# Attention and two feed-forward layers on one core: per-row factors spread by TensorE in the first pairs, Newton steps for the inverse root, weight words joined as integers, paced transfers

## The chip, the core and the metric

The kernel runs on one core of one Trainium2 chip. A core has five engines with an instruction queue each: TensorE (matrix products), VectorE, ScalarE, GpSimd, and SyncE, which here issues every transfer between memory and the on-chip buffers. In the rows they are called PE, DVE, ACT, POOL and SP; PEld is TensorE's weight load. Each engine works through its own instructions in the order in which they were written, and waits where an operand is not there yet. The metric is the device time of one execution in microseconds (us), as the median of several runs.

## What is computed

```
attention: 4 batches x 12 heads, 448 positions, head size 64
  q_n, k_n = rmsnorm(q, g_q), rmsnorm(k, g_k)       # x / sqrt(mean(x*x) + 1e-6) * g
  p = exp(s - max(s)),  s = q_n k_n^T / 8
  p = p / (sum(p) + 1e-9);  a = p v
x = a as 1792 rows of 768
x = relu(x @ w_in)**2 @ w_out                        # hidden size 2048
x = (silu(x @ w_gate) * (x @ w_val)) @ w_out2        # hidden size 1536
```

## The kernel before

**Attention.** Two heads of 448 rows are taken together as a pair and cut into 7 row tiles of 128; there are 24 pairs, six to a batch. For a pair the kernel loads k and q transposed (`kq`), scales k by its norm and by the gains, splits k and q each into a rounded part and a rest (`kst`, `kst_lo`, `qst`, `qst_lo`), and forms the scores of a tile with three products (`sc`, L678). VectorE takes the row maxima (L706) and forms the exponent's bias (`m`, L707); ScalarE takes the exponential and the row sum (`ring`, L720); TensorE turns the tile (`pt`, L777), a copy takes it out of PSUM (`turned_p`), and when all seven are there, eight products with v make the pair's output (`o`, L809). VectorE multiplies it by the inverse row sums (`ox`, L826). Pairs are numbered from 0, so o of pair 4 is the fifth.

**Norms.** `row_sums` loads the natural rows (`nat`), squares them and sums them (`ss`, L470). `rsqrt` makes the inverse root: VectorE adds the constant (L435) and GpSimd raises to the power -0.5 (L441), once for k (`stage`) and once for q (`rms`), for one or two pairs at a time. The factors of k lie along partitions but are needed along the free axis in all 128 partitions. For pair 0 TensorE turns them (`rows`, L557) and spreads them with a selecting matrix `pick` (`rk`, L522). For all other pairs they go to memory (`rkd`, L499) and are read back into 128 partitions (`rkb`, L602). The inverse row sums take the same way (`zd` L750, `zb` L758).

**Weights.** Every weight arrives as 64-bit words, of which the kernel makes a 32-bit number, and from that a rounded part and a rest. A half tile of 128 x 384 (a chunk) takes these steps in `load_weights`: scale the high word (`wa`, ScalarE or VectorE), then on VectorE a shift (L279), sign and bits joined (L282), exponent bits masked (L285), low word times exponent (L288), the sum (L292, VectorE or GpSimd), then the rounded part and the rest (`lo`, L305). There are 136 chunks, 24 of them for the first six blocks of the first layer, decoded during attention.

**Feed-forward.** Each product is three matrix products of 448 columns (L318). As soon as a batch's attention is done, parts of the first layer (`h_a`, `ya`) fill gaps between the attention's instructions (rank FILL); they are 702 matrix products in all, with the last batch's `lead`. After attention the sweeps of `products()` follow, which hold nothing but feed-forward work; between sweeps x is read back in six tiles, one after another (`xr`, L1042, then ScalarE's copy and VectorE's subtraction L1045).

**What sets the order.** The Python code plays a schedule before it writes instructions: every step is a generator that names the engines it could run on with a planned cost in ns; W is a VectorE step that shares a port with GpSimd, G a GpSimd step, S a transfer. `dispatch` hands each engine, whenever its planned clock is free, the ready job of lowest rank. So a changed cost or step moves all later instructions, on every engine, and a step that may run on two engines can change its engine. The two PSUM banks f0 and f1 are lent to attention until `LEND` tiles have their exponentials, and are then given to the filling work.

Of the kernel before, what the change touches and what calls it, by code (L numbers as in the profile page):

```python
# [9 lines left out]
F32 = mybir.dt.float32  # L10
# [18 lines left out]
EPS_SUM = 1e-9  # L29
RING = 6  # L30
LEND = 28
# [33 lines left out]
SIGN_EXP_BITS = -(1 << 23)  # L65
# [4 lines left out]
def attention_two_ffn_kernel(  # L70
# [112 lines left out]
    def dispatch(e):  # L183
# [15 lines left out]
        if e == "S":  # L199
            dma_free[0] = max(dma_free[0], clock[0] + 1100) + p[2] / 360  # L200
            done = dma_free[0] + 900
        else:
            done += p[2] if len(p) > 2 else settle[e]
# [9 lines left out]
    def dma(issue, nbytes):  # L213
        yield DMA_MARGIN
        yield {"S": 475}, issue, nbytes
# [34 lines left out]
    def load_weights(items):  # L250
# [7 lines left out]
        def chunk(key, place, c, raw_at):  # L258
# [33 lines left out]
            yield {"W": 469, "G": 956}, lambda e: e.tensor_tensor(out=t, in0=t, in1=a, op=ALU.add)  # L292
# [114 lines left out]
    pick = xp.tile([128, 2 * S], F32, tag="x5", name="pick")[:PT].rearrange("p (t m) -> p t m", t=PT)  # L407
    nc.gpsimd.memset(pick, 0.0)
    for i in range(PT):
        nc.gpsimd.affine_select(  # L410
            out=pick[:, i, :], in_=pick[:, i, :], compare_op=ALU.not_equal, fill=1.0, base=-i,
            pattern=[[0, 128]], channel_multiplier=1,
        )
# [16 lines left out]
    power = ap.tile([128, 2, PT], F32, name="power")  # L430
    nc.gpsimd.memset(power, -0.5)

    def rsqrt(ss, ends):

        yield {"W": 150}, lambda e: e.tensor_scalar(  # L435
            out=ss, in0=ss, scalar1=1.0 / D, scalar2=EPS_RMS, op0=ALU.mult, op1=ALU.add
        )
# [13 lines left out]
    def stat_tiles(b):  # L451
        for name, tag in (("ss", f"ss{b % 2}"), ("rms", f"rms{b % 2}")):
            stat[name, b] = ap.tile([128, 2, PB, PT], F32, tag=tag, name=f"{name}{b}")
# [29 lines left out]
    def stats(b, p, n):  # L483
# [4 lines left out]
        yield lambda: ("ss", b) in stat  # L488
# [4 lines left out]
        y, ss = (stat[name, b][:, :, p:p + n] for name in ("rms", "ss"))  # L493
        yield lambda: stage_free
        at = stage_free.pop(0)
        yield from rsqrt(ss, [(stage[at][:, :n * PT].rearrange("p (r t) -> p r t", t=PT), 0), (y[:, 1], 1)])
# [6 lines left out]
    def first_stats():  # L503
# [7 lines left out]
        rows, rows_at = yield from k_rows(0, 0, 1, 0)  # L511
        yield lambda: t_banks
        where = t_banks.pop(0)
        rk = tile_at(where, [128, S], F32, "rk")

        def broadcast(e):
            for h in range(2):
                at = 0
                while at < S:
                    i, c = divmod(h * S + at, 128)  # L520
                    w = min(128 - c, S - at)
                    e.matmul(  # L522
                        rk[64 * h:64 * h + 64, bass.ds(at, w)], lhsT=pick[:, i, :64], rhs=rows[:, c:c + w],
                        start=True, stop=True,
                    )
                    at += w

        yield {"P": 1500}, broadcast, 0
        spawn(first_k(rk, where), -95, True)
        rkr_free.append(rows_at)  # L530

    def row_sums_then(gen, w):
        yield from gen
        y, ss = (stat[name, 0][:, w, 0] for name in ("rms", "ss"))
        yield from rsqrt(ss, [(y if w else stage[0][:, :PT], None)])
        summed.add(w)
        if w:
            rms_ready.add(0)

    def first_k(rk, where):  # L540
        yield settle["P"]
        yield lambda: 0 in raw_kq and gained
        k = raw_kq[0][:, :S]
        yield {"W": 596}, lambda e: e.scalar_tensor_tensor(
            out=k, in0=k, scalar=gqk, in1=rk, op0=ALU.mult, op1=ALU.mult
        )
        ks[0] = [k]
        t_banks.append(where)

# [11 lines left out]
    ks, qs, vs, raw_kq, kq_at = {}, {}, {}, {}, {}  # L561
# [5 lines left out]
    def feed():  # L567

        for g in range(NH // 2):
# [17 lines left out]
            raw_kq[g] = kq if g in PLAIN else 2  # L587
# [5 lines left out]
            spawn(load_rk(g, kq[:, :S]), rank, True)  # L593
# [141 lines left out]
    def norms(g):  # L735
# [12 lines left out]
        sum_free.append(at)  # L748
        yield 200
# [69 lines left out]
    def pair_outputs(g, o, o_at):  # L819

        yield settle["P"]
        yield lambda: ox_free and g in zinv
# [4 lines left out]
        t_banks.append(o_at)  # L827
        zb_free.append(zb_at)
# [404 lines left out]
```

## Time and profile before

| | before |
|---|---|
| median of 3 runs, us | 1331.65 (1327.26 to 1337.62) |
| the profiled execution, us | 1334.34 |
| its span on the core, us | 1332.5 |
| TensorE busy, us and share of the span | 1281.5, 96% |
| VectorE busy | 756.2, 57% |
| ScalarE busy | 577.9, 43% |
| GpSimd busy | 196.4, 15% |
| mean granted TensorE clock | 0.985 |

The shares are means over stages that differ. In the first 200 us VectorE and ScalarE are close to full and TensorE has gaps; later TensorE hardly ever stops. Busy time of TensorE is not useful time: at the half clock a product is busy for longer, and matrix products overlap, so that their busy time is longer than their spacing.

### The profile page before, as it was taken

What the parts mean: (1) busy time and instruction counts of PE and PEld (TensorE: products, weight loads), DVE (VectorE), ACT (ScalarE), POOL (GpSimd) and SP (SyncE); (2) the same over time, 40 slices, a digit from 0 to 9 for tenths busy, and PEclk for the clock granted to TensorE, in tenths of its full rate; (3) what the DMA queues carried; (4) which work ended last, traced back from release to release, by engine and by line L of the source; (5) the groups of instructions that cost most, each with busy time, mean ns of one, the idle gap of its engine ahead of it and who ended that gap; (6) DMA issues with size and microseconds to landing.
All of it is one profiled execution on the core that took longest, in us unless ns stands there. A gap on an engine that the chain in (4) does not pass through costs nothing.

```text
span 1332.5 us, 18347 instructions
## 1 busy us (share of the span) xinstructions
PE 1281.5 (96%) x6565; PEld 1079.2 (81%) x6565; DVE 756.2 (57%) x1568; ACT 577.9 (43%) x1260; POOL 196.4 (15%) x156
## 2 busy tenths in 40 slices
PE   8888998999999999999999989999999999999998
PEld 5455555667668899999999979999999999999998
DVE  6888995455432899947943588221229961213122
ACT  6887887666763444523522243121215431211110
POOL 6674554433201000000000000000000000000000
PEclk9997999999999999999999989999999999999999
DMA  6565655432310544654453356120105420303021
GB/s 215 175 197 152 188 160 163 152 102 84 101 60 21 166 143 132 206 171 137 150 186 98 126 176 182 37 83 1 63 0 188 144 81 1 104 0 111 15 84 42
DMA packets 87421, 153.10 MB, mean 115 GB/s; under 512 B 15385, under 2 KB 66914, under 8 KB 87330
## 3 DMA queue, kind: packets, MB, share of 16 engines
q1 hardware_dynamic: 87330, 151.93, 36.9%
q8 instruction: 52, 0.85, 0.3%
q14 instruction: 39, 0.32, 0.1%
HBM read 122.82 MB, written 29.07 MB: 114 GB/s over the span
## 4 chain that ended last, share of the span: by engine, by line
PE 72%; DMA 3%; DVE 2%; ACT 1%; issue 1%; SPq 0%; POOL 0%; DVEq 0%; ACTq 0%
PE y L318 25%; PE h_v L318 13%; PE h_g L318 13%; PE h L318 11%; PE h_a L318 3%; PE ya L318 2%; PE pt L777 2%; PE o L809 2%; PE sc L678 1%; DMA xr<-x2d 1%; DMA raw_in<-in_w_in_dram 1%; DMA nat<-in_q_n_dram 0%; ACT ring L720 0%; DMA raw_out<-in_w_out_dram 0%; DMA zb<-zd 0%
## 5 line engine op out<-in xcount | busy, mean ns | idle before, releaser
L318 PE MATMUL h_g<-x,hi_g 128*128 128x448 f32 x576 | 165.2, 368 | 5.9 <-ACT x L209 5.9
L318 PE MATMUL h_v<-x,hi_v 128*128 128x448 f32 x576 | 165.8, 369 | 0.0
L318 PE MATMUL y<-s,hi_o 128*128 128x448 f32 x576 | 164.1, 366 | 0.0
L318 PE MATMUL y<-s,hi_out 128*128 128x448 f32 x552 | 159.3, 370 | 3.1 <-DVE r L355 3.1
L720 ACT ACTIVATE ring<-sc,m,rms 128x448 f32<-128x448 f32 x168 | 122.8, 733 | 58.8 <-PE pt L777 45.4
L318 PE MATMUL h<-x,hi_in 128*128 128x448 f32 x516 | 147.4, 367 | 0.0
L371 DVE TENSOR_TENSOR sig<-h_g,sig 128x448 f32<-128x448 f32 x48 | 29.9, 623 | 189.1 <-ACT sig L370 189.0
L777 PEld LDWEIGHTS pt<-ident,ring 128*128 128x128 f32 x672 | 75.4, 145 | 68.9 <-ACT turned_p L209 26.1
L777 PE MATMUL pt<-ident,ring 128*128 128x128 f32 x672 | 108.1, 291 | 21.1 <-ACT turned_p L209 11.7
L318 PEld LDWEIGHTS h_g<-x,hi_g 128*128 128x128 f32 x576 | 108.3, 188 | 15.8 <-ACT x L209 6.2
L706 DVE TENSOR_REDUCE sc<-sc 128x1 f32<-128x448 f32 (+1 forms) x96 | 93.8, 977 | 42.1 <-PE sc L678 36.1
L318 PEld LDWEIGHTS h_v<-x,hi_v 128*128 128x128 f32 x576 | 109.3, 190 | 9.5
L318 PEld LDWEIGHTS y<-s,hi_o 128*128 128x128 f32 x576 | 108.1, 188 | 9.3
L318 PEld LDWEIGHTS y<-s,hi_out 128*128 128x128 f32 x552 | 105.1, 191 | 12.5 <-DVE r L355 3.5
L370 ACT ACTIVATE sig<-h_g 128x448 f32<-128x448 f32 x48 | 26.2, 545 | 191.7 <-PE h_g L318 191.4
L318 PE MATMUL h_v<-x,lo_v 128*128 128x448 f32 x288 | 106.0, 368 | 0.0
L318 PE MATMUL h_g<-x,lo_g 128*128 128x448 f32 x288 | 105.6, 367 | 0.0
L318 PE MATMUL y<-s,lo_o 128*128 128x448 f32 x288 | 105.4, 366 | 0.0
L318 PEld LDWEIGHTS h<-x,hi_in 128*128 128x128 f32 x516 | 96.9, 188 | 8.6
L318 PE MATMUL y<-s,lo_out 128*128 128x448 f32 x276 | 101.9, 369 | 0.0
L209 ACT COPY turned_p<-pt 128x512 f32<-128x512 f32 x165 | 94.0, 588 | 5.2 <-PE pt L777 5.1
L318 PE MATMUL h<-x,lo_in 128*128 128x448 f32 x258 | 94.5, 366 | 0.0
(157 smaller groups left out, 2283.7 us busy)
## 6 DMA issues: line engine op xcount, KB each, us to landing
raw_in<-in_w_in_dram SPq DMA_DIRECT2D x32, 384.0 KB
raw_out<-in_w_out_dram SPq DMA_DIRECT2D x32, 384.0 KB
kq<-in_kq_p_dram SPq DMA_DIRECT2D x23, 480.0 KB
xr<-x2d SPq DMA_DIRECT2D x42, 224.0 KB
raw_g<-in_w_gate_dram SPq DMA_DIRECT2D x24, 384.0 KB
raw_v<-in_w_val_dram SPq DMA_DIRECT2D x24, 384.0 KB
raw_o<-in_w_out_dram SPq DMA_DIRECT2D x24, 384.0 KB
xr<-x1d SPq DMA_DIRECT2D x36, 224.0 KB
```

Source lines behind the costliest of these rows:

```text
L209: e.copy(out, src)
L318: return {"P": 203}, lambda e: e.matmul(ps, lhsT=w, rhs=x, start=first, stop=last), 0
L370: yield {"A": 424}, lambda e: e.activation(out=t, in_=pg, func=ACTF.Sigmoid)
L371: yield {"V": 535}, lambda e: e.tensor_tensor(out=t, in0=pg, in1=t, op=ALU.mult)
L678: e.matmul(parts[t][:, :S], lhsT=q[a][d, bass.ts(i % 4, 128)], rhs=k[c][d], start=(p == 0), stop=(p == len(passes) - 1),)
L706: e.tensor_reduce(out=top, in_=sc, axis=AX.X, op=ALU.max, negate=True)
L720: yield {"A": 704}, lambda e: e.activation(out=probs(at + t), in_=parts[t][:, :S], func=ACTF.Exp, bias=m[:, t:t + 1], scale=rq[:, i:i + 1] ...
L777: e.transpose(ps[:, bass.ts(j, 128)], p[:, bass.ds(min(128 * j, S - 128), 128)], ident)
L809: e.matmul(o[64 * h:64 * h + 64], lhsT=v[:, 4 * h + j], rhs=turned_p[:, 2 * j + h], start=(j == 0), stop=(j == 3),)
```

## The change

1. `SPREAD_K = 5`, `SPREAD_Z = 5`: the norms of k and the inverse row sums of pairs 0 to 4 are spread by TensorE with `pick` (now 14 rows wide) into a PSUM bank, and don't go through memory. `spread`, `spread_k` and `first_k` do it. For these pairs the output is first copied out of PSUM (`ox<-o`), so that its bank comes free before the factors are there.
2. `rsqrt` no longer raises to a power on GpSimd: it begins from an integer estimate and takes three Newton steps, all on VectorE for pairs 0 to 2 (three groups, `fused`: L436 to L451), otherwise with the beginning on VectorE and the steps on GpSimd (13 small instructions).
3. A chunk's words are joined as integers: the low word is scaled to its top three bits (L286), sign joined (L290), the high word shifted in (L293). The mask, the product and the sum are gone. The raw buffer is free after L286, and the sum can no longer go to GpSimd.
4. The planner's transfer rate goes from 360 to 300, and a transfer of 150000 bytes or more is not issued while the planned queue is more than 600 ns ahead. `LEND` goes from 28 to 35: one pair later.

```diff
-LEND = 28
+LEND = 35
+SPREAD_K = 5
+SPREAD_Z = 5
+DMA_RATE = 300
+DMA_BULK = 150000
+DMA_QUEUE = 600
...
     def dma(issue, nbytes):
         yield DMA_MARGIN
+        while nbytes >= DMA_BULK and dma_free[0] > clock[0] + 1100 + DMA_QUEUE:
+            yield dma_free[0] - clock[0] - 1100 - DMA_QUEUE
         yield {"S": 475}, issue, nbytes
...
             yield {"W": 269}, lambda e: e.tensor_scalar(
-                out=ti, in0=ai, scalar1=3, scalar2=None, op0=ALU.logical_shift_left
+                out=ti, in0=raw[:, :, 0].bitcast(U32), scalar1=2.0 ** -29, scalar2=7.0, op0=ALU.mult, op1=ALU.min
             )
+            raws.append(raw_at)
             yield {"W": 469}, lambda e: e.scalar_tensor_tensor(
                 out=ti, in0=ai, scalar=SIGN_BIT, in1=ti, op0=ALU.bitwise_and, op1=ALU.bitwise_or
             )
-            yield {"W": 269}, lambda e: e.tensor_scalar(
-                out=ai, in0=ti, scalar1=SIGN_EXP_BITS, scalar2=None, op0=ALU.bitwise_and
+            yield {"W": 469}, lambda e: e.scalar_tensor_tensor(
+                out=ti, in0=ai, scalar=3, in1=ti, op0=ALU.logical_shift_left, op1=ALU.bitwise_or
             )
-            yield {"W": 469}, lambda e: e.scalar_tensor_tensor(
-                out=a, in0=raw[:, :, 0].bitcast(U32), scalar=2.0 ** -52, in1=a, op0=ALU.mult, op1=ALU.mult
-            )
-            raws.append(raw_at)
-            yield {"W": 469, "G": 956}, lambda e: e.tensor_tensor(out=t, in0=t, in1=a, op=ALU.add)
             was.append(a_at)
...
-        for dst, part in ends:
-            src = ss if part is None else ss[:, part]
-            to = power[:, 0] if part is None else power[:, :src.shape[1]]
-            yield {"G": 900}, lambda e: e.tensor_tensor(out=dst, in0=src, in1=to, op=ALU.pow)
+        if fused:
+            def all_steps(e):
+                begin(e)
+                for i in range(3):
+                    step(e, ends if i == 2 else [(y, None)])
+
+            yield {"W": 170 * (10 + len(ends))}, all_steps
+            return
+        yield {"W": 300}, begin
+        for i in range(3):
+            yield {"G": 900}, lambda e: step(e, ends if i == 2 else [(y, None)])
...
-        yield from dma(lambda e: e.dma_start(out=rk_d[b][p * PT:(p + n) * PT, :], in_=rows), 0)
+        for r in range(n):
+            if b * PB + p + r < SPREAD_K:
+                yield from spread_k(b * PB + p + r, rows, r)
+        if b * PB + p + n > SPREAD_K:
+            yield from dma(lambda e: e.dma_start(out=rk_d[b][p * PT:(p + n) * PT, :], in_=rows), 0)
...
+    def spread(rows, parts, name):
+
         yield lambda: t_banks
         where = t_banks.pop(0)
-        rk = tile_at(where, [128, S], F32, "rk")
+        ps = tile_at(where, [128, S], F32, name)
...
+        yield {"P": 1100}, broadcast, 0
+        return ps, where
...
+        if g < SPREAD_Z:
+            parts = [(4 * h + t, 0, 128, h, 128 * t) for t in range(3) for h in range(2)]
+            parts += [(3, 64 * h, 64, h, 384) for h in range(2)]
+            zinv[g] = yield from spread(rows, parts, f"zb{g}")
+            zr_free.append(zr_at)
+            return
...
+        if g < SPREAD_Z:
+            yield {"A": 467, "V": 535}, lambda e: copy(e, ox, o)
+            t_banks.append(o_at)
+            o = ox
+            yield lambda: g in zinv
         zb, zb_at = zinv.pop(g)
         yield {"V": 535}, lambda e: e.tensor_tensor(out=ox, in0=o, in1=zb, op=ALU.mult)
```

What this does to the written order is seen at three places.

TensorE, from the last turned tile of pair 0 to pair 0's product with v, before (`sum` holds the inverse row sums, `stage` the k factors of later pairs; the first product of pair 1 stands behind o):

```order
L777 MATMUL pt_508<-ident,ring 128x128 x4
L557 MATMUL rows<-ident,sum_255 128x128
L557 MATMUL rows<-ident,stage_257 128x128
L809 MATMUL o_539<-turned_p,v_247 64x448 x8
L678 MATMUL sc_565<-kst_529,qst_361 128x448
```

The same stretch of TensorE in the change, from the second group of pair 1's scores (sc_572) on:

```order
L722 MATMUL sc_572<-kst_485,qst_455 128x448 x2
L722 MATMUL sc_572<-kst_lo_486,qst_455 128x448 x2
L722 MATMUL sc_572<-kst_485,qst_lo_456 128x448 x2
L600 MATMUL rows<-ident,sum_274 128x128
L827 MATMUL pt_573<-ident,ring 128x128 x4
...
L551 MATMUL zb_616<-zr_588,pick 64x128 x6
L551 MATMUL zb_616<-zr_588,pick 64x64 x2
...
L859 MATMUL o_633<-turned_p,v_268 64x448 x8
```

Three of the four groups of pair 1's scores have moved ahead of pair 0's output, and so have the spread factors of pair 0 (`zb`) and those of pairs 1 to 3 (`rk`, eight products each).

VectorE at the start, before: the sums of squares of pairs 0 to 2 up to the scaling of pair 0's k (L544) and the first maximum (L706).

```order
L470 TENSOR_REDUCE ss_263<-nat_0_265 128x7
L435 TENSOR_SCALAR ss_263<-ss_263 128x7
L977 TENSOR_SCALAR gqk<-g 128x1
...
L544 SCALAR_TENSOR_TENSOR kq_267<-kq_267,gqk,rk 128x448
L470 TENSOR_REDUCE ss_263<-nat_0_273 128x7
L706 TENSOR_REDUCE sc_372<-sc_372 128x1
```

VectorE at the start of the change: the first of three fused chains, that of pair 0's k.

```order
L494 TENSOR_REDUCE ss_282<-nat_0_285 128x7
L436 TENSOR_SCALAR ss_282<-ss_282 128x7
L437 TENSOR_SCALAR rms_284<-ss_282 128x7
L442 TENSOR_TENSOR rst_283<-rms_284 128x7
L444 SCALAR_TENSOR_TENSOR rst_283<-rst_283,ss_282 128x7
L451 SCALAR_TENSOR_TENSOR rms_284<-rst_283,rms_284 128x7
...
L451 SCALAR_TENSOR_TENSOR stage_276<-rst_283,rms_284 128x7
```

Ahead of the first maximum VectorE has 12 instructions before and 42 now; what came in belongs to the three chains.

VectorE near the end of the first layer, before, between the subtractions for the first two of six x tiles that the second layer begins with (x_6_0, x_6_1):

```order
L1045 TENSOR_TENSOR x_6_0_7977<-xr_6_0_7954,x_6_0_7977 128x448
L292 TENSOR_TENSOR wt_v_0_7942<-wt_v_0_7942,wa_v_0_7911 128x384
L305 TENSOR_TENSOR lo_g_7983<-wt_g_0_7862,hi_g_7982 128x384
L355 SCALAR_TENSOR_TENSOR r_6_13_7988<-h_6_13_7947,r_6_13_7988 128x448
L288 SCALAR_TENSOR_TENSOR wa_g_1_7254<-raw_g_1_7227,wa_g_1_7254 128x384
L359 TENSOR_TENSOR s_6_13_7987<-r_6_13_7988,s_6_13_7987 128x448
L279 TENSOR_SCALAR wt_v_1_8012<-wa_v_1_7932 128x384
L292 TENSOR_TENSOR wt_g_1_7920<-wt_g_1_7920,wa_g_1_7254 128x384
L305 TENSOR_TENSOR lo_v_8029<-wt_v_0_7942,hi_v_8028 128x384
L282 SCALAR_TENSOR_TENSOR wt_v_1_8012<-wa_v_1_7932,wt_v_1_8012 128x384
L1045 TENSOR_TENSOR x_6_1_8039<-xr_6_1_8001,x_6_1_8039 128x448
```

The same stretch in the change:

```order
L1101 TENSOR_TENSOR x_6_0_8050<-xr_6_0_7998,x_6_0_8050 128x448
L362 TENSOR_TENSOR s_6_13_8030<-r_6_13_8031,s_6_13_8030 128x448
L290 SCALAR_TENSOR_TENSOR wt_v_1_8041<-wa_v_1_7955,wt_v_1_8041 128x384
L286 TENSOR_SCALAR wt_o_0_8073<-raw_o_0_8010 128x384
L308 TENSOR_TENSOR lo_v_8076<-wt_v_0_7964,hi_v_8075 128x384
L290 SCALAR_TENSOR_TENSOR wt_o_0_8073<-wa_o_0_8066,wt_o_0_8073 128x384
L293 SCALAR_TENSOR_TENSOR wt_v_1_8041<-wa_v_1_7955,wt_v_1_8041 128x384
L293 SCALAR_TENSOR_TENSOR wt_o_0_8073<-wa_o_0_8066,wt_o_0_8073 128x384
L286 TENSOR_SCALAR wt_o_1_8092<-raw_o_1_8013 128x384
L308 TENSOR_TENSOR lo_v_8076<-wt_v_1_8041,hi_v_8075 128x384
L290 SCALAR_TENSOR_TENSOR wt_o_1_8092<-wa_o_1_8084,wt_o_1_8092 128x384
L1101 TENSOR_TENSOR x_6_1_8107<-xr_6_1_8068,x_6_1_8107 128x448
```

A chunk has become shorter, but parts of three chunks now stand between the two x tiles instead of parts of two. From the last square ahead of the six x tiles to the sixth x tile VectorE has 57 rows before and 65 now.

## Rows read from the trace of the kernel before

**Rows 1.** Stretches: length, then busy us (instructions) of PE, PEld, DVE, ACT, POOL; clock; DMA share, GB/s.

```profile
0.00:20.00 20.00, 17.12 (x105) 12.70 (x105) 12.44 (x27) 12.75 (x28) 14.26 (x30) 1.00 0.68 224
20.00:40.00 20.00, 14.40 (x75) 7.53 (x73) 14.40 (x30) 12.98 (x33) 8.55 (x6) 0.91 0.63 173
40.00:100.00 60.00, 50.20 (x293) 30.32 (x292) 52.37 (x110) 52.07 (x128) 44.24 (x30) 0.99 0.65 194
100.00:194.40 94.40, 82.41 (x461) 53.15 (x459) 88.43 (x177) 79.17 (x188) 43.67 (x29) 0.91 0.58 170
194.40:430.00 235.60, 227.43 (x1306) 157.86 (x1304) 107.47 (x205) 153.49 (x366) 74.40 (x55) 0.99 0.32 97
430.00:480.00 50.00, 46.88 (x218) 42.67 (x217) 41.09 (x97) 22.14 (x46) 1.19 (x1) 0.93 0.53 159
480.00:1333.00 853.00, 843.06 (x4120) 774.92 (x4118) 440.00 (x927) 245.27 (x479) 10.08 (x8) 0.99 0.32 101
```

**Rows 2.** TensorE's waits from 0 to 470 us: waiter, releaser, total us, times, longest.

```profile
PE pt L777 <- ACT turned_p L209: 11.7, 12, 1.9
...
PE y L318 <- DVE r L355: 3.1, 1, 3.1
```

**Rows 3.** Chain that ended last, to 480 us: start, us, work (matrix records).

```profile
377.84 1.02 PE pt L777 x8
...
379.48 0.80 PE sc L678 x6
...
411.11 3.16 PE o L809 x16
414.27 11.55 PE h_a L318 x56
```

**Rows 4.** TensorE in order of time: start, us, work, idle before it and releaser.

```profile
7.46 1.48 PE L522 MATMUL rk<-rkr,pick 7*64 7x128 f32 x16
...
91.30 3.23 PE L809 MATMUL o<-turned_p,v 128*64 128x448 f32 x16
...
98.06 0.36 PE L678 MATMUL sc<-kst,qst_lo 64*128 64x448 f32 x2
...
102.09 0.58 PE L678 MATMUL sc<-kst,qst_lo 64*128 64x448 f32 x2
...
215.53 3.23 PE L809 MATMUL o<-turned_p,v 128*64 128x448 f32 x16
...
793.17 1.40 PE L318 MATMUL h_g<-x,hi_g 128*128 128x448 f32 x2 [5.87 <-ACT x L209]
```

**Rows 5.** VectorE to 470 us by shape: count, busy us, mean ns, idle before it.

```profile
L282 DVE SCALAR_TENSOR_TENSOR wt_in<-wa_in,wt_in 128x384 int32<-128x384 int32 x20 | 12.6, 636 | 0.0
...
L292 DVE TENSOR_TENSOR wt_in<-wt_in,wa_in 128x384 f32<-128x384 f32 x15 | 11.3, 758 | 0.0
...
L288 DVE SCALAR_TENSOR_TENSOR wa_in<-raw_in,wa_in 128x384 f32<-128x384 uint32 x19 | 11.1, 588 | 0.0
...
L292 DVE TENSOR_TENSOR wt_out<-wt_out,wa_out 128x384 f32<-128x384 f32 x16 | 8.5, 549 | 0.0
...
L435 DVE TENSOR_SCALAR ss<-ss 128x28 f32<-128x28 f32 x11 | 2.5, 227 | 0.1
...
L271 DVE TENSOR_SCALAR wa_out<-raw_out 128x384 f32<-128x384 f32 x2 | 0.7, 366 | 0.5 <-DMA raw_out<-in_w_out_dram 0.5
```

**Rows 6.** VectorE in order of time.

```profile
24.71 1.18 DVE L624 SCALAR_TENSOR_TENSOR kq<-kq,gqk,rkb 128x448 f32<-128x448 f32 x1 [2.35 <-DMA raw_in<-in_w_in_dram]
...
37.93 0.62 DVE L826 TENSOR_TENSOR ox<-o,zb 128x448 f32<-128x448 f32 x1
...
194.41 0.16 DVE L707 TENSOR_TENSOR m<-sc,rms 128x2 f32<-128x2 f32 x1
```

**Rows 7.** GpSimd to 470 us by shape, columns as in rows 5.

```profile
L441 POOL TENSOR_TENSOR rms<-ss,power 128x14 f32<-128x14 f32 x11 | 29.4, 2676 | 0.0
...
L465 POOL TENSOR_TENSOR nat<-nat 128x448 f32<-128x448 f32 x18 | 18.4, 1024 | 21.6 <-DMA nat<-in_k_n_dram 13.2 <-DMA nat<-in_q_n_dram 8.2
```

**Rows 8.** ScalarE to 470 us by shape, columns as in rows 5.

```profile
L209 ACT CAST x<-ox 128x448 fp32r<-128x448 f32 x24 | 13.5, 564 | 10.9 <-DVE ox L826 8.0 <-PE h_a L318 2.9
```

More of the change, by code (lines that the diff above doesn't have):

```diff
@@ L428, in attention_two_ffn_kernel, with rsqrt, begin, step @@
     rows_ready = set()
[L430 to L437, printed above, removed]
[L438 to L441 removed]
+    def rsqrt(y, ss, t, ends, fused):
+        def begin(e):
+            e.tensor_scalar(out=ss, in0=ss, scalar1=1.0 / D, scalar2=EPS_RMS, op0=ALU.mult, op1=ALU.add)
+            e.tensor_scalar(
+                out=y.bitcast(I32), in0=ss.bitcast(I32), scalar1=-0.5, scalar2=RSQRT_MAGIC, op0=ALU.mult, op1=ALU.add
+            )
+        def step(e, to):
+            e.tensor_tensor(out=t, in0=y, in1=y, op=ALU.mult)
+            if fused:
+                e.scalar_tensor_tensor(out=t, in0=t, scalar=-0.5, in1=ss, op0=ALU.mult, op1=ALU.mult)
+            else:
+                e.tensor_tensor(out=t, in0=t, in1=ss, op=ALU.mult)
+                e.tensor_scalar(out=t, in0=t, scalar1=-0.5, scalar2=1.5, op0=ALU.mult, op1=ALU.add)
+            for dst, part in to:
+                a, b = (t, y) if part is None else (t[:, part], y[:, part])
+                if fused:
+                    e.scalar_tensor_tensor(out=dst, in0=a, scalar=1.5, in1=b, op0=ALU.add, op1=ALU.mult)
+                else:
+                    e.tensor_tensor(out=dst, in0=a, in1=b, op=ALU.mult)
+        if fused:
+            def all_steps(e):
[7 more added lines that the diff above has]
+            yield {"G": 900}, lambda e: step(e, ends if i == 2 else [(y, None)])
     stat, halves = {}, {}
@@ L511, in first_stats, with spread_k @@
         rows, rows_at = yield from k_rows(0, 0, 1, 0)
+        yield from spread_k(0, rows, 0)
+        rkr_free.append(rows_at)
+    def spread(rows, parts, name):
         yield lambda: t_banks
         where = t_banks.pop(0)
-        rk = tile_at(where, [128, S], F32, "rk")
+        ps = tile_at(where, [128, S], F32, name)
         def broadcast(e):
-            for h in range(2):
[L518 to L530, printed above, removed]
+            for i, c, w, h, at in parts:
+                e.matmul(
+                    ps[64 * h:64 * h + 64, bass.ds(at, w)], lhsT=pick[:rows.shape[0], i], rhs=rows[:, c:c + w],
+                    start=True, stop=True,
+                )
+        yield {"P": 1100}, broadcast, 0
+        return ps, where
+    def spread_k(g, rows, r):
+        yield lambda: g in kq_tile
+        parts = []
+        for at in range(0, S, 64):
+            for h in range(2):
+                i, c = divmod(h * S + at, 128)
+                w = min(128 - c, S - at)
+                if at == 0 or c == 0:
+                    parts.append((r * PT + i, c, w, h, at))
+        rk, where = yield from spread(rows, parts, f"rk{g}")
+        spawn(first_k(g, rk, where), PT * g - STATS_LEAD if g else -95, True)
     def row_sums_then(gen, w):
         yield from gen
-        y, ss = (stat[name, 0][:, w, 0] for name in ("rms", "ss"))
-        yield from rsqrt(ss, [(y if w else stage[0][:, :PT], None)])
+        y, ss, t = (stat[name, 0][:, w, 0] for name in ("rms", "ss", "rst"))
+        yield from rsqrt(y, ss, t, [(y if w else stage[0][:, :PT], None)], True)
         summed.add(w)
@@ L538, in row_sums_then, with first_k @@
             rms_ready.add(0)
-    def first_k(rk, where):
+    def first_k(g, rk, where):
         yield settle["P"]
-        yield lambda: 0 in raw_kq and gained
-        k = raw_kq[0][:, :S]
+        yield lambda: gained
+        kr = kq_tile[g][:, :S]
         yield {"W": 596}, lambda e: e.scalar_tensor_tensor(
-            out=k, in0=k, scalar=gqk, in1=rk, op0=ALU.mult, op1=ALU.mult
+            out=kr, in0=kr, scalar=gqk, in1=rk, op0=ALU.mult, op1=ALU.mult
         )
-        ks[0] = [k]
         t_banks.append(where)
+        if g in PLAIN:
+            ks[g] = [kr]
+            return
+        ks[g] = yield from split(g, kr, "kst", S)
+        release_kq(g)
     rms_ready = set()
```

33 lines of the change are left out of this document (18 added, 15 removed).

## Prediction

> **What bounds the kernel now.** I read the stretches first [rows 1]. From 480 us on TensorE has 4120 records in 853 us and is busy for 843 of them: this part is a queue of matrix products and ends when they do. From 194 to 480 us TensorE is busy for 227.4 of 235.6 and 46.9 of 50 us. The gaps lie in the first 194.4 us. To see how large they are, busy time won't do, so I take spacings from the chain [rows 3]: 56 feed-forward records in 11.55 us are 0.206 us each, the sixteen records of an output 3.16, eight turning products (two tiles) 1.02, six score products 0.80. A pair has 7 tiles and 21 score products, so 7 x 0.51 + 21 x 0.134 + 3.16 = about 9.5 us of TensorE. Between the outputs of pairs 4 and 11 lie 124.2 us [rows 4]; seven pairs are 67 us, and the 129 filling products that the order has there 27. So 30 us of these 124 are lost, some to waits on copies (11.7 us in all) [rows 2], some to the clock: it is 0.91 in that stretch [rows 1], and the same two products take 0.36 us at 98 us and 0.58 at 102 [rows 4].
>
> Who sets the pace there? VectorE is busy for 12.4, 14.4, 52.4 and 88.4 us of 20, 20, 60 and 94.4 [rows 1]: 167.7 of 194.4, with 26.7 us idle, 20.8 of them in the first 100 us. ScalarE has 157 us. The last maximum of pair 11 ends that stretch [rows 6]. After it VectorE is half empty. So I price the change by the time at which VectorE gets past this maximum, then by what TensorE has behind it or still before it.
>
> **The words as integers.** Counted in the order up to that maximum, VectorE loses 24 low-word products, 20 sums and 25 masks or scalings and gains 28 joins and one conversion. A join or a product takes about 0.62 us, the mean of 0.636 and 0.588; a sum 0.65, between 0.758 and 0.549; a scalar operation 0.37 [rows 5]. That is 14.9 + 13.0 + 9.2 - 17.4 - 0.4 = 19.3 us less. The conversion L286 reads every second word, which nothing in the first steps did on VectorE but L271, at 0.366 us: I take that. If it ran like a join, 26 of them would give back 6.5 us.
>
> **Newton.** To the same place VectorE gains 48 small instructions. The nearest row is the 28-column scalar operation at 0.227 us [rows 5], so at most 10.9 us; a bare 0.16, as the small product at 194 us takes [rows 6], gives 7.7. I take 9.5. [...] On GpSimd, two powers of about 2.68 us each go [rows 7], and 13 small instructions come. Their nearest rows are 0.227 us on another engine and 1.024 us for 448 columns: 3 to 13 us against 5.4. I take 4. GpSimd is busy for under half of the stretches from 20 us on except the third, where it has 44 of 60 us, so this hides, but at 13 us a group the factors of pairs 2 to 5 would be late by some 8 us each time.
>
> **What moves onto VectorE.** With new costs the planner also gives VectorE ten more full-width instructions up to that maximum (copies, subtractions, scalings that ScalarE or GpSimd had): 10 x 0.6 = 6 us. Together: -19.3 + 9.5 + 6 = about -4 us; from -1 (small ones at 0.227, ten at 0.7) to -7. VectorE thus has 164 us of work before the maximum, hardly less than before: most of what the words free is spent again.
>
> **Spreading by TensorE.** This removes the ways through memory for five pairs. It shows in VectorE's idle time: pair 1's scaling of k starts at 24.71 us, 2.35 us idle ahead of it, and pair 0's output is multiplied only at 37.93 [rows 6]. Now three of four score groups of pair 1 stand ahead of pair 0's output on TensorE. Of the 26.7 us idle, 3.9 lie before VectorE's first operand and stay; of the other 3.7 in the first 20 us I keep 1, of 5.6 up to 40 us 2, of 7.6 up to 100 us 4, of 6.0 after that 6. That leaves 17. The maximum comes at 164 + 17 = 181 us, 13.5 earlier. TensorE can follow: from pair 4 to pair 11 it would need 67 + 168 x 0.206 = 102 us, and gets about 115.
>
> The price: nine more spreads. Sixteen records took 1.48 us [rows 4], so 13 us as busy time at most and 9 x 0.75 = 7 as I read the overlap; they lie in a time in which TensorE is idle for a sixth to a quarter, so I cost them at 0. Without this cover they would cost 7. Five more copies on ScalarE are 5 x 0.564 = 2.8 us [rows 8], hidden in its gaps of 7 and 8 us per 20. The start gets worse: VectorE has 42 instructions ahead of the first maximum instead of 12, 30 x 0.2 = 6 us, of which about 3 fall on idle time. That is in the 181 already.
>
> **Filling work.** At the output of pair 11 the order has 168 filling products done instead of 150. These 18 x 0.206 = 3.7 us come off what TensorE still has to do. (Before pair 4's output it is the other way round: none instead of 21, by `LEND`.)
>
> **Later.** Between 430 and 480 us TensorE waits 3.1 us for VectorE, ahead of its first product with a square [rows 1, 2]; VectorE has 42 instructions instead of 46 between the last pair's output and the first square, worth 1 to 2 us: -1. At 793 us it waits 5.87 us for the six x tiles [rows 4]. There VectorE has 65 rows instead of 57 ahead of the last tile, at about 0.5 us: up to +4; I take +2.
>
> **Paced transfers.** In the order the load of pair 1's kq moves behind two weight loads, one place further for each; 30 issues fewer stand on SyncE's queue. DMA is busy for 0.58 to 0.68 there [rows 1], so I cost it at nothing; were a weight chunk late, VectorE would pass over nothing and wait, at most a few us.
>
> **Sum.** -13.5 - 3.7 - 1 + 2 = -16.2 us on the profiled execution's 1334.3: 1318. That execution lies 2.7 us above the median of the runs, 1331.65, so the forecast is **1315 us**, a little over 1% faster, 1% being about what a measurement of this kernel can tell from no change.
>
> **Rivals.**
> - *VectorE's relief arrives whole.* Its idle time falls to 8 us, the half clock between 100 and 130 us goes, and so does the wait between 430 and 480 us with the slow stretch behind it (3.1 us, and 0.07 of 50 by the clock, 6 us in all) [rows 1, 2]. Then -22.5 - 3.7 - 6 = 1300. For it: 30 of 124 us lost there. Against it: ScalarE too has 157 us of work.
> - *Nothing arrives.* The idle time stays 26, since ScalarE and the tile copies set the pace [rows 2]; only the 4 us of VectorE's work and the 3.7 of filling work are left, and the x tiles take 4 back: about 1328.
> - *Slower: the half clock takes hold early.* TensorE has no filling work until pair 5, where it had 21 products; if it falls to the lower level from pair 1 to pair 4, its 40 us of work there take 0.58 / 0.36 of that, 64 us, and it, no longer VectorE, sets the pace at 16 us a pair. Some 12 us over what VectorE needs, and with what follows late 18: about 1335; where it stays low up to pair 7, 1350. It decides by the clock in 40 to 100 us: now 0.99. [...]
> - *The paced loads or the x tiles cost more than the start gains*: a new wait of 5.9 us at two or three of the later x loads, 1330.
> - *The change doesn't do what it says*: the conversion at a join's price over all chunks, or slow small steps on GpSimd: 1325 to 1330.
>
> **Chances.** Forecast 0.45 (own range 1307 to 1322), whole relief 0.17, nothing 0.15, later waits or slow steps 0.10, half clock 0.13. Faster by over 1% (below 1318.3): 0.17 and three quarters of 0.45, 0.5. Slower by over 1% (above 1345): a good half of the half clock and a rest, 0.1. Within 1%: 0.4. The range 1297 to 1337 leaves out the ends of the first rival and the long half clock, less than 2 in 10.
>
> **What would show it.** Right: pair 11's last maximum near 181 us, VectorE idle about 17 us before it, small Newton steps at 0.2 us, L286 near 0.37, TensorE's clock at 1.0 to 100 us, o of pair 11 near 202. Wrong: the clock at half before 100 us; L286 above 0.5 us; x tiles that come later than 5.9 us; a wait of VectorE on a raw load.

## The result

| | before | after |
|---|---|---|
| median of 15 runs, us | 1332.83 (1326.25 to 1339.46) | 1319.8 (1314.85 to 1325.88) |
| ratio, 95% interval | | 0.9902 [0.9884, 0.9921] |
| span of the profiled execution, us | 1332.5 | 1315.5 |
| VectorE / ScalarE / GpSimd busy, us | 756.2 / 577.9 / 196.4 | 671.0 / 568.4 / 153.3 |
| start of o of pairs 4, 6, 9, 11, us | 91.30, 131.66, 177.80, 215.53 | 84.30, 118.41, 174.47, 210.35 |
| start of o of pairs 16, 23, us | 295.32, 411.04 | 282.93, 395.77 |

The change is 13 us faster in the medians, 0.98%, inside the range and 5 us above the forecast of 1315. The two profiled executions lie 17 us apart; single executions of one kernel scatter by some 6 us to either side, so what follows rests on medians for times, and on traces for places.

The change is 13.2 us ahead at o of pair 6, has lost 10 of them by pair 9, and gains another 10 between pairs 11 and 23 (15.3 ahead there). The stretches of after, cut at the last maximum of pair 11 (189.2 us), with the columns of [rows 1]:

```profile
0.00:20.00 20.00, 17.65 (x115) 14.25 (x117) 14.76 (x51) 10.46 (x22) 7.82 (x32) 0.91 0.61 203
20.00:40.00 20.00, 18.15 (x140) 11.75 (x136) 17.34 (x38) 17.81 (x44) 10.98 (x27) 0.91 0.71 224
40.00:100.00 60.00, 52.97 (x391) 33.95 (x391) 56.26 (x124) 56.09 (x140) 29.15 (x40) 1.00 0.60 178
100.00:189.20 89.20, 79.35 (x453) 52.86 (x450) 74.53 (x148) 68.89 (x166) 38.24 (x61) 0.96 0.57 171
189.20:430.00 240.80, 237.69 (x1360) 167.95 (x1359) 112.68 (x217) 156.78 (x374) 63.95 (x96) 0.99 0.34 103
430.00:480.00 50.00, 47.45 (x226) 43.19 (x225) 47.54 (x107) 31.27 (x65) 0.00 (x0) 0.97 0.70 214
480.00:1316.00 836.00, 826.00 (x4035) 758.33 (x4033) 347.86 (x686) 227.13 (x447) 3.14 (x3) 1.00 0.30 97
```

VectorE's work up to that maximum is 14.76 + 17.34 + 56.26 + 74.53 = 162.9 us, where 164 was forecast; its idle time is 26.3, where 17 was. Up to 100 us it idles 11.6 us (20.8 before); behind that 14.7 (6.0 before). What it waits for there, in after, from 117 to 189 us (waiter, releaser, total us, times, longest):

```profile
DVE sc L750 <- PE sc L722: 8.1, 5, 3.2
DVE sum L783 <- ACT ring L764: 2.6, 1, 2.6
...
```

TensorE's waits in after from 0 to 470 us, in the same form, beside [rows 2]:

```profile
PE sc L722 <- ACT ring L764: 8.8, 12, 1.8
...
PE y L321 <- DVE r L358: 2.3, 1, 2.3
...
PE pt L827 <- ACT turned_p L214: 1.0, 2, 0.8
```

The kernel before has this line for the scores:

```profile
PE sc L678 <- ACT ring L720: 5.3, 8, 1.1
```

The waits on the tile copies are nearly gone (1.0 for 11.7), those of the scores on the exponentials have grown from 5.3 to 8.8. The shapes that were priced without a row of their own, as VectorE (first) and GpSimd ran them in after to 470 us (columns of [rows 5]):

```profile
L290 DVE SCALAR_TENSOR_TENSOR wt_out<-wa_out,wt_out 128x384 int32<-128x384 int32 x24 | 15.2, 641 | 0.3
...
L293 DVE SCALAR_TENSOR_TENSOR wt_out<-wa_out,wt_out 128x384 int32<-128x384 int32 x23 | 12.6, 551 | 0.0
...
L286 DVE TENSOR_SCALAR wt_in<-raw_in 128x384 int32<-128x384 uint32 x24 | 10.4, 442 | 0.0
L286 DVE TENSOR_SCALAR wt_out<-raw_out 128x384 int32<-128x384 uint32 x24 | 8.8, 372 | 0.0
...
L442 DVE TENSOR_TENSOR rst<-rms 128x7 f32<-128x7 f32 x6 | 1.0, 167 | 0.2
...
L442 DVE TENSOR_TENSOR rst<-rms 128x28 f32<-128x28 f32 x3 | 0.6, 189 | 0.1
```

```profile
L442 POOL TENSOR_TENSOR rst<-rms 128x28 f32<-128x28 f32 x30 | 10.2, 340 | 26.3 <-DVE rms L437 25.4
...
L447 POOL TENSOR_SCALAR rst<-rst 128x28 f32<-128x28 f32 x30 | 7.9, 265 | 2.6
```

### The profile page after: what moved, and what is told of

Its sections match the earlier page's. It is cut to its first block, busy times and chain, and to the rows that moved or that the text cites. A ratio compares the mean times of both kernels' runs of the same rounds, so it can differ in the third digit from the quotient of the medians.

```text
span 1315.5 us, 18513 instructions
## 1 busy us (share of the span) xinstructions
PE 1279.3 (97%) x6709; PEld 1082.3 (82%) x6709; DVE 671.0 (51%) x1366; ACT 568.4 (43%) x1251; POOL 153.3 (12%) x256
## 4 chain that ended last, share of the span: by engine, by line
PE 70%; DVE 2%; DMA 1%; ACT 1%; issue 0%; SPq 0%; DVEq 0%; ACTq 0%
PE y L321 26%; PE h_v L321 14%; PE h_g L321 13%; PE h L321 12%; PE h_a L321 2%; PE ya L321 1%; PE o L859 1%; PE pt L827 1%; DMA xr<-x2d 1%; PE sc L722 1%; DMA raw_in<-in_w_in_dram 0%; DVE lo_out L308 0%; DVE wt_out L290 0%; DVE wt_out L293 0%; DVE wt_in L290 0%
## 5 line engine op out<-in xcount | busy, mean ns | idle before, releaser
L827 PEld LDWEIGHTS pt<-ident,ring 128*128 128x128 f32 x672 | 73.7, 142 | 50.3 <-ACT turned_p L214 11.6
L827 PE MATMUL pt<-ident,ring 128*128 128x128 f32 x672 | 102.7, 283 | 6.9 <-ACT ring L764 3.0
```

The lines of the kernel that those rows point to most:

```text
L827: e.transpose(ps[:, bass.ts(j, 128)], p[:, bass.ds(min(128 * j, S - 128), 128)], ident)
```

## The experiments

Theory A is the prediction's: VectorE's work up to pair 11's last maximum sets the pace. Theory B: from pair 6 or 7 on TensorE and the copies set it. A third came up late: GpSimd's powers hold transfers back.

**One part undone at a time.** In each of these the planner makes a new order for what is left, so every engine's instructions stand elsewhere too. The four ran together (10 runs each, 31 of the kernel before, 1330.56 us).

*Words*: the five old steps of a chunk in place of L286 to L293.

```diff
...
-out=ti, in0=raw[:, :, 0].bitcast(U32), scalar1=2.0 ** -29, scalar2=7.0, op0=ALU.mult, op1=ALU.min
+out=ti, in0=ai, scalar1=3, scalar2=None, op0=ALU.logical_shift_left
...
+out=ai, in0=ti, scalar1=SIGN_EXP_BITS, scalar2=None, op0=ALU.bitwise_and
...
-out=ti, in0=ai, scalar=3, in1=ti, op0=ALU.logical_shift_left, op1=ALU.bitwise_or
+out=a, in0=raw[:, :, 0].bitcast(U32), scalar=2.0 ** -52, in1=a, op0=ALU.mult, op1=ALU.mult
...
+yield {"W": 469, "G": 956}, lambda e: e.tensor_tensor(out=t, in0=t, in1=a, op=ALU.add)
```

> The change with the weight words decoded as before (mask, product and sum back), all else kept; the planner writes its order anew. Up to the last maximum of pair 11 VectorE then has about 14 us more work. Theory A, VectorE sets the pace up to there: that maximum comes 8 to 14 us later than in the change (189 us), and the whole is 8 to 12 us slower, about 1330. Theory B, TensorE has taken over from pair 7 on: the maximum of pair 7 comes 5 to 8 us later but that of pair 11 only 2 to 4, and the whole is 2 to 5 us slower, about 1323.

Measured: 1320.89 us, 0.9926 [0.9898, 0.9954]; pair 11's last maximum at 192.73 us (189.19 in the change).

*Newton*: `rsqrt` of the kernel before.

```diff
-        yield {"W": 300}, begin
-        for i in range(3):
-            yield {"G": 900}, lambda e: step(e, ends if i == 2 else [(y, None)])
...
+        for dst, part in ends:
...
+            yield {"G": 900}, lambda e: e.tensor_tensor(out=dst, in0=src, in1=to, op=ALU.pow)
```

> The change with the power on GpSimd instead of Newton steps. VectorE has about 10 us less work up to the last maximum of pair 11 (3 of them before the first maximum), GpSimd two powers of 2.7 us per group instead of 13 small steps. Theory A (VectorE sets the pace): 5 to 9 us faster, about 1312. Theory B (TensorE and the tile copies set it from pair 7): first outputs 2 to 3 us earlier, the whole within 2 us of the change. Third: the factors come later by the second power, and the first pairs lose what VectorE gains, 2 to 4 us slower.

Measured: 1325.2 us, 0.9965 [0.994, 0.999]; maximum at 197.09 us. The stretch from 20 to 40 us, where TensorE falls to its lower level for longer (granted clock 0.74; 0.91 in the change):

```profile
20.00:40.00 20.00, 18.57 (x120) 11.71 (x121) 14.34 (x28) 13.77 (x35) 14.14 (x8) 0.74 0.45 142
```

*Spreads* and *pacing*: the constants alone.

```diff
-SPREAD_K = 5
-SPREAD_Z = 5
+SPREAD_K = 1
+SPREAD_Z = 0
```

> The change with SPREAD_K = 1 and SPREAD_Z = 0, as before: only pair 0's k factors are spread by TensorE, the others and the inverse sums go through memory. VectorE's work up to pair 11 is the same to 1 us. My prediction's step: its idle time grows by 3 to 6 us before 40 us and by 3 more up to 100 us, the output of pair 4 starts 5 to 8 us later than at 84 us, the whole is 4 to 8 us slower. Rival: the waits only move, and the whole is within 2 us.

Measured: 1321.07 us, 0.9938 [0.9916, 0.996]; the last maximum of pair 2 at 60.87 us (51.87 in the change), of pair 11 at 198.21. VectorE's wait for a factor that comes back from memory is there again, from 0 to 60 us 3.7 us (0.6 in the change):

```profile
DVE kq L668 <- DMA rkb<-rkd: 3.7, 2, 3.4
```

```diff
-DMA_RATE = 300
-DMA_BULK = 150000
+DMA_RATE = 360
+DMA_BULK = 1 << 40
```

> The change with DMA_RATE = 360 and no pacing of large transfers. Theory P, the 10 us gained between the outputs of pairs 11 and 23 come from pacing (before, small transfers of inverse sums stood behind large ones): they are lost again, about 1328 to 1330, with TensorE gaps near 280 to 300 us. Rival: pacing only moves loads that nobody waits for, within 2 us of the change, and the later gain comes from the faster words.

Measured: 1321.12 us, 0.9924 [0.99, 0.9948]; maximum at 194.20 us.

What follows: undoing Newton costs most, the spreads next; for words and pacing the intervals overlap that of the change, that of the spreads touches it. Undoing the words gives VectorE 173.6 us of work up to pair 11's maximum instead of 162.9, and that maximum moves by 3.5 us. Taking Newton back gives it 156.3, and the maximum comes 8 us later. So the times don't follow VectorE's work. For the words it came as Theory B expected (pair 7 at 122.27 for 116.84, then less at pair 11).

The gain between pairs 11 and 23 is still there in all four: from last maximum to last maximum they take 190.1 (words), 184.9 (Newton), 190.4 (spreads) and 187.7 us (pacing); the change takes 190.1 and the kernel before 200.0. So no single one of the four is needed for it, the pacing least of all. `LEND`, which changed with them, was not undone.

**The change with more work on one engine, order unchanged.** Each of the next three writes one kind of instruction more often without a word to the planner; every other instruction stands where it stands in the change.

```diff
...
-            yield {"W": 469}, lambda e: e.scalar_tensor_tensor(
...
+            more = len(seen) < 24
+            seen.append(key)
+
+            def sign(e):
+                for _ in range(2 if more else 1):
+                    e.scalar_tensor_tensor(
+                        out=ti, in0=ai, scalar=SIGN_BIT, in1=ti, op0=ALU.bitwise_and, op1=ALU.bitwise_or
+                    )
+
+            yield {"W": 469}, sign
```

> The change with one instruction written twice: the join of the sign, for the first 24 chunks, without a word to the planner, so every engine's order stays as in the change. VectorE gets 22 more full-width instructions of 0.6 us up to the last maximum of pair 11: 13 us more work there, 15 us in all. Theory A (VectorE sets the pace up to pair 11): that maximum comes 10 to 13 us later than 189.2 and the end 8 to 13 us later, 1328 to 1333. Theory B (from pair 6 on TensorE and the copies on ScalarE set the pace, VectorE's 26 us of idle time take the work up): the maximum comes at most 3 us later, and the time stays within 3 us of the change, 1317 to 1323.

```diff
...
+            more = len(seen) < 24
+            seen.append(key)
...
+                    for _ in range(2 if more else 1):
+                        e.activation(out=a, in_=raw[:, :, 1].bitcast(F32), func=ACTF.Copy, scale=2.0 ** -112)
...
```

> The change with ScalarE's scaling of the high words written twice for the first 24 chunks, order otherwise as in the change: 22 more instructions of 0.56 us, 12 us more work for ScalarE between pairs 2 and 11. Theory A: ScalarE is hidden, at most 3 us. Theory B: ScalarE was busy in the hole between 117 and 140 us and ahead of the tile copies, so 5 to 10 us of the 12 arrive at the last maximum of pair 11 and at the end: 1325 to 1330.

```diff
...
+                        for r in range(3 if p == 0 and 5 <= g <= 11 else 1):
+                            e.matmul(
+                                parts[t][:, :S], lhsT=q[a][d, bass.ts(i % 4, 128)], rhs=k[c][d],
+                                start=(p == 0), stop=(p == len(passes) - 1 or (p == 0 and 5 <= g <= 11 and r < 2)),
+                            )
```

> The change with the first score product of each tile of pairs 5 to 11 written three times (each starts the sum anew, so the scores are the same), order otherwise as in the change: 98 more matrix products of 0.133 us, 13 us more work for TensorE between 85 and 200 us. Theory A (TensorE waits for VectorE there): hidden, o of pair 11 and the end at most 4 us later. Theory B: o of pair 11 comes 9 to 13 us later than 210.35 and the end too, 1329 to 1333.

> The change itself once more, as the reference of the other three: 1320 us, 0.990 of the kernel before.

| work added up to pair 11's maximum | that maximum, us | of pair 23 | median, us | ratio to before |
|---|---|---|---|---|
| none (the change again) | 190.45 | 378.25 | 1318.92 | 0.9891 [0.9868, 0.9913] |
| VectorE 24 joins, 14 us | 212.02 | 401.62 | 1340.49 | 1.0059 [1.0037, 1.0081] |
| ScalarE 12 us | 199.01 | 388.70 | 1326.4 | 0.9943 [0.9914, 0.9972] |
| TensorE 13 us | 196.01 | 385.98 | 1324.07 | 0.9934 [0.9913, 0.9954] |

Theory B, that VectorE has 26 us to spare, falls: its additions came out as 21.6 us at the maximum and 21.6 at the end, more than Theory A expected too. All 24 joins lie ahead of that maximum, not 22. The 26 us are waits in front of instructions that others wait for in turn, not time to fill. From the start to pair 11's last maximum, the change again and then extra_vector (columns of [rows 1]):

```profile
0.00:190.45 190.45, 168.93 (x1093) 112.84 (x1094) 162.56 (x359) 153.45 (x368) 85.55 (x158) 0.96 0.59 181
```

```profile
0.00:212.02 212.02, 178.58 (x1093) 117.50 (x1094) 183.99 (x383) 154.44 (x368) 89.31 (x158) 0.92 0.53 163
```

VectorE's busy time grew by 21.4 us and its idle time not at all (27.9 and 28.0). Of the 21.4 the 24 joins are 14; the rest is that other instructions of VectorE lasted longer. TensorE's clock is lower there as well, 0.86 from 40 to 100 us where the change has 1.00; that the clock cost time beyond VectorE's 21.4 is not shown. In extra_vector from 40 to 100 us:

```profile
40.00:100.00 60.00, 50.44 (x323) 29.68 (x323) 51.86 (x108) 44.98 (x111) 23.13 (x26) 0.86 0.48 145
```

But ScalarE's and TensorE's additions arrive too, for about 0.6 and 0.4 of their size. Theory A alone does not say that.

**Less work on VectorE, order unchanged.** The counter-test, in the change and in the kernel before: the join of the sign is left out for 24 chunks.

```diff
...
+            skip = len(seen) < 24
+            seen.append(key)
-            yield {"W": 469}, lambda e: e.scalar_tensor_tensor(
+            yield {"W": 469}, lambda e: None if skip else e.scalar_tensor_tensor(
...
```

> The change without the join of the sign for the first 24 chunks, left out without a word to the planner, so every engine's order stays as in the change (those weights lose their signs; the time is read for the work alone). VectorE has 22 instructions or 13.2 us less up to the last maximum of pair 11. If VectorE's work still sets the pace in the change as extra_vector says (13 us more work came out as 17 us there and 21 at the end): the maximum at 176 to 180 us and the end 9 to 15 us earlier, about 1307. If TensorE has taken over and only added work hurts: the maximum no more than 4 us earlier, 1316 or more.

Measured: 1316.4 us, 0.9888 [0.9854, 0.9922] (the change again: 0.9891); maximum at 188.36 us instead of 190.45, with 13.2 us less of VectorE's work ahead of it. (The 17 us that the expectation names were read one maximum too early; it is 21.6.)

> The kernel before without the join of the sign for the first 24 chunks, order as in the kernel before (weights lose their signs; the time is read for the work alone). VectorE has 13.2 us less up to the last maximum of pair 11, about what the prediction made of the relief. If VectorE's work up to that maximum was the bound, as the prediction said: 194.4 becomes 181 to 184 us, and the time 1318 to 1322, a ratio of 0.990. If waits set the pace there: 190 or later, and a ratio of 0.995 or more.

Measured: 1329.37 us, 0.9979 [0.996, 0.9998]. From pair 7 on its maxima are those of before: 129.64 us (129.70), pair 11 194.29 (194.41), pair 15 260.64 (260.73), pair 23 394.48 (394.42). The stretch from 140 to 194.4 us in the kernel before, and then in this one:

```profile
140.00:194.40 54.40, 48.72 (x297) 32.14 (x295) 52.75 (x106) 47.98 (x115) 25.86 (x19) 1.00 0.59 181
```

```profile
140.00:194.40 54.40, 51.10 (x301) 34.13 (x302) 48.92 (x101) 48.64 (x118) 26.35 (x19) 0.97 0.63 186
```

VectorE has 3.8 us less to do in this stretch and reaches its end at the same time. Up to pair 11's last maximum it is busy for 10.9 us less (156.7 for 167.6). The first pairs of this execution ran up to 4 us late (pair 5 at 96.69 instead of 92.61), which was made up by pair 7; from there to pair 11 both kernels take 64.7 us, with 57.2 and 63.0 us of VectorE's work. This is the run that decides on counting VectorE's work one for one: its relief, taken alone, is worth 2.2 us in the kernel before, and nothing clear of the noise in the change, not 13. Work added to VectorE is paid in full and work taken away gives next to nothing. That VectorE, ScalarE and TensorE are close together there, and hand work to each other in a fixed order, fits this, but which of them ends each wait was not followed.

**An order drawn again.** The planner's transfer rate 305 instead of 300.

```diff
-DMA_RATE = 300
+DMA_RATE = 305
```

> The change with the planner's transfer rate 305 instead of 300: no work changes, but a tenth of the instructions stand in another order. This is the measure for the runs that undo one part, which all make a new order too. If an order that is only drawn again costs nothing: 1317 to 1322, 0.990. If the undone parts' 3 to 5 us were mostly such redrawn orders: 1322 to 1327.

Measured: 1317.24 us, 0.9892 [0.9867, 0.9917]. One redrawn order costs nothing that shows here, so the 5 to 8 us of Newton and spreads are likely not that; a single draw doesn't bound the scatter of others. Pair 11's last maximum did move, to 186.10 us, so shifts of 3 to 4 us at that place, as with words and pacing, can come from the order alone.

**GpSimd's powers taken out of the kernel before.**

```diff
-yield {"G": 900}, lambda e: e.tensor_tensor(out=dst, in0=src, in1=to, op=ALU.pow)
+yield {"G": 900}, lambda e: e.tensor_tensor(out=dst, in0=src, in1=to, op=ALU.add)
```

> The kernel before with each power on GpSimd replaced by one addition on the same operands (the norms are wrong; the time is read for the work alone), order as in the kernel before: some 25 powers of 1.5 to 2.7 us become 0.3 us, about 55 us less for GpSimd. If the powers hold back TensorE there (at 273.6 to 279.9 us two of them delay kst_lo, for which SyncE waits 6.0 us with a load of pair 16's inverse sums behind it, and TensorE stops for 2.7 us at 283 us): that stop goes, 2 to 4 us, pair 0's first maximum comes 2 to 3 us earlier and the factors of pairs 2 to 5 too, together 6 to 12 us, a ratio of 0.991 to 0.9955. If they are hidden, as the prediction took them: within 2 us of the kernel before, 0.9985 to 1.0.

Measured: 1327.88 us, 0.9959 [0.9935, 0.9983], 5.7 us less. How a power on GpSimd reaches TensorE is seen in the kernel before at 273 us. GpSimd in order of time (start, us, work):

```profile
273.57 2.58 POOL L441 TENSOR_TENSOR stage<-ss,power 128x14 f32<-128x14 f32 x1 [2.25 <-PE sc L678]
276.11 1.27 POOL L611 TENSOR_TENSOR qst_lo<-kq,qst 128x512 fp32r<-128x512 f32 x1
277.34 2.59 POOL L441 TENSOR_TENSOR rms<-ss,power 128x14 f32<-128x14 f32 x1
279.89 1.15 POOL L611 TENSOR_TENSOR kst_lo<-kq,kst 128x448 fp32r<-128x448 f32 x1
```

SyncE's longest wait in the kernel before between 268 and 292 us, and the issue that follows the load:

```profile
SPq L574 <- POOL kst_lo L611: 6.0, 1, 6.0
...
281.46 0.45 SPq L758 DMA_DIRECT2D zb<-zd  x1
```

VectorE in order of time there, then TensorE (in brackets the idle time ahead and its releaser):

```profile
285.10 0.62 DVE L826 TENSOR_TENSOR ox<-o,zb 128x448 f32<-128x448 f32 x1 [3.16 <-DMA zb<-zd]
```

```profile
285.78 0.33 PE L557 MATMUL rows<-ident,sum 128*128 128x128 f32 x1 [2.71 <-DVE ox L826]
...
287.41 0.58 PE L678 MATMUL sc<-kst_lo,qst 64*128 64x448 f32 x2
```

The second power ends at 279.9 us, `kst_lo` behind it at 281.0. SyncE may issue the load of the next kq (L574) only then, for which it has waited 6.0 us, and the last third of a pair's inverse sums (`zb`) stands behind that load on its queue. VectorE has its output late, TensorE stops for 2.7 us and then runs the same products at 0.58 instead of 0.37 us. Without the powers this stop is gone: SyncE waits 2.0 us there, and from pair 16's last maximum to pair 17's it takes 16.4 us instead of 20.6. The stretch from 250 to 320 us in the kernel before, then in the kernel before without its powers, then in the change:

```profile
250.00:320.00 70.00, 66.84 (x385) 45.04 (x382) 36.58 (x70) 47.23 (x113) 24.10 (x16) 0.98 0.37 115
```

```profile
250.00:320.00 70.00, 69.20 (x403) 46.91 (x402) 36.87 (x72) 49.00 (x118) 16.77 (x18) 1.00 0.38 120
```

```profile
250.00:320.00 70.00, 69.71 (x399) 47.72 (x399) 37.68 (x73) 48.35 (x116) 24.42 (x40) 1.00 0.35 108
```

In the change the same place reads so on GpSimd, where the steps are short (`kst_lo` starts at 268.43, 3.9 us behind pair 16's last maximum; 5.1 before):

```profile
264.79 0.65 POOL L453 TENSOR_TENSOR rms<-rst,rms 128x28 f32<-128x28 f32 x1
265.40 1.29 POOL L655 TENSOR_TENSOR qst_lo<-kq,qst 128x512 fp32r<-128x512 f32 x1
...
268.43 1.14 POOL L655 TENSOR_TENSOR kst_lo<-kq,kst 128x448 fp32r<-128x448 f32 x1
```

SyncE still waits there, but in the new order all three loads of `zb` stand ahead of the load of kq:

```profile
SPq L617 <- POOL kst_lo L655: 4.4, 1, 4.4
...
263.40 1.73 SPq L808 DMA_DIRECT2D zb<-zd  x3
269.59 0.34 SPq L617 DMA_DIRECT2D kq<-in_kq_p_dram  x1
```

So in the change it is the order of issue that keeps this wait away from TensorE, and not the short steps alone. With the powers back in a new order (the run *Newton* above) TensorE does not stop there either, although SyncE waits 6.5 us for `kst_lo`.

The start did not follow the expectation: pair 0's last maximum came where it did (19.46 and 19.47 us), and pair 11's last maximum came at 198.31, later than before. All of that run's gain comes after it: 194.6 us from there to pair 23's, where the kernel before takes 200.0. At pair 23 it is 1.6 us ahead (392.86 for 394.42); the other 4.6 of the 6.2 us between the two profiled spans come later, where neither kernel has a power, and are not explained.

## Why the prediction came out as it did

- **The time was right, its main term was not.** -13.5 us were to come from VectorE getting past pair 11's last maximum at 181 instead of 194.4. It got there at 189.2, and o of pair 11 started at 210.35 (5.2 earlier), not near 202. The step that failed is "who sets the pace there? VectorE": its work was counted right (162.9 us for 164), but that count plus a guessed rest of idle time didn't set the time. With 10.9 us less of it the kernel before reached the maximum at the same place, and the undone words, 10.7 us more, moved it by 3.5. High busy time, 167.7 of 194.4, was read as the bound, though ScalarE had 157 and TensorE 164.
- **That the sum came out is luck.** In the profiled executions -13.5 up to pair 11, -3.7 by filling work and +1 later were forecast, -16.2 in all. Measured were -5.2 up to o of pair 11, -10.1 from there to o of pair 23, and -1.7 behind it, -17.0 in all. What was missing up to pair 11 came back later from causes that the sum doesn't have.
- **Idle time of 17 us.** The first 100 us went as forecast, 11.6 us idle (3.9 + 1 + 2 + 4 = 10.9). After that 6 was the forecast and 14.7 came, 8.1 of it waits for TensorE's scores from 117 to 189 us. TensorE "would need 102 us, and gets about 115" from pair 4's to pair 11's output; it took 126. The low end of -7 for VectorE's work doesn't follow from the terms either, which give -5.6 with the small steps at 0.16.
- **Later gains, not in the sum.** Between the outputs of pairs 11 and 23 the change is 10.1 us quicker. 3.3 of them are the filling work that was done before (318 products left instead of 334, by 0.206): the -3.7 of the prediction, counted again, not tested alone. Most of the rest are stops such as that at 283 us: between these outputs TensorE waits 4.8 us in the kernel before, and for the change the view lists no wait. The prediction never looked for them, since TensorE had little idle time there in a mean over 235 us. In the kernel before from 218 to 411 us:

```profile
PE rows L557 <- DVE ox L826: 3.0, 2, 2.7
PE pt L777 <- DVE ox L826: 1.5, 1, 1.5
PE pt L777 <- ACT turned_p L209: 0.3, 1, 0.3
```

- **Newton on GpSimd** was costed at nothing, "this hides". As durations this was right: 13 steps take 3.8 us a group (three times 340 + 295 + 265 ns, two of 291, 248 and 235), 4 were taken, against 5.4 for the powers. But the powers were not hidden. Taken out alone they give 5.7 us, put back alone, in a new order, they cost 5.4 by the medians (1325.2 for 1319.8, in different sessions) and 8 by the ratios (0.9965 and 0.9902). The two act at different places: out of the old order, behind pair 11, at 283 us above all; back in the new one, before pair 11, which comes 8 us later. Going by these numbers it is the largest single part of the gain that the runs show.
- **Spreads** at 0 as a price, and VectorE's early waits gone: right, with 9 us at pair 2 and about 5 at the end (by the ratios; 1.3 by the medians), both with the spreads undone. **Pacing** at 0: its undoing moved the time by less than the intervals tell.
- **L286** at 0.366: 0.442 and 0.372 up to 470 us, but 0.37 over all 136 chunks, as priced. **Newton on VectorE** at 0.2 a step: 0.165 to 0.19 for the products; the two scalar operations that begin a group took 0.27 each on 28 columns. Four times the columns added 0.022 us to a product (0.167 on 7, 0.189 on 28), so at these sizes nearly all of its time does not follow the columns.
- **430 to 480 us**: the wait fell from 3.1 to 2.3 us, -1 was forecast. **The x tiles**: +2 was forecast, but 5.5 and 0.2 us stand for 5.87.
- **The rivals.** Clock at half before 100 us: it was 0.91, 0.91 and 1.00 (the kernel before has 0.50 from 100 to 103 us). In the run with more work on VectorE the clock did fall there, to 0.86, but its 21.6 us are VectorE's own added busy time. "Nothing arrives" was, for VectorE's relief alone, the right rival.

What stays open: what sets the pace of the kernel before from pair 7 to 11, where 5.7 us less on VectorE changed nothing; which share the words have (at most some 3 us by their undoing); which part, if any, brings the gain between pairs 11 and 23, since it stays when any one of four is undone; what `LEND` does; and why the run without powers is late at pair 11 and gains 4.6 us behind pair 23. Newton's steps written into the old order, or powers into the new one, were not tried.

## What to carry to other kernels

An engine that is busy for 86% of a stretch is not yet its bound while others are at 81 and 84%: before a relief is counted one for one, take a part of the work out at an unchanged order and look whether the next milestone moves. A long instruction on an engine that is mostly idle still costs time if a buffer waits for what stands behind it, above all where a load for that buffer holds up a whole transfer queue (here a power of 2.59 us on GpSimd, which is busy for 15%, a wait of 6.0 us on SyncE's queue and a stop of 2.7 us for TensorE). And a mean over a long stretch hides single stops: a list of TensorE's waits there, followed back through SyncE's queue, would have shown the one at 283 us ahead of time. Work added tests something else than work taken away: here additions to VectorE were paid in full, and the counterpart gave next to nothing. When work is added, look at the engine's busy time too, which grew by 21.4 us for 14 us of additions.

## What the runs showed of the hardware

A power on GpSimd is dear for itself: 2676 to 2715 ns for 128x14 in the kernel before, where an addition of the same shape took 238 to 322 ns in the same place; on 128x7 a power 1481 to 1490, an addition 202 to 204. Short GpSimd products on 128x28 take 291 to 340 ns, against 186 to 189 on VectorE; a scalar operation of that shape takes about the same on both (265 and 270). A VectorE instruction can last longer beside one of GpSimd: in the change, up to pair 11, the ten of VectorE's single full-width instructions other than maxima and sums that took over 0.85 us all started while a GpSimd instruction ran (a join at 92.29 us took 1.5 us, beside `x<-ox,x` from 91.78 to 93.37; such joins take 0.55 to 0.73 in the mean). In the kernel before, up to 470 us, the 28 sign joins (L282) that started while no GpSimd instruction ran took 0.54 to 0.56 us, the ten others 0.55 to 1.49. That is seen in the traces, not tested; the planner's `port`, which W steps and GpSimd's steps take in turns, is a rule of the plan that stands for such durations. TensorE's mean granted clock was 0.983 with the joins added to VectorE, and 0.992 without.
